# Retention and MLP on one core: the MLP's first layer by another seven-product form, with first products copied into PSUM banks

## The chip, the cores and the metric

The kernel runs on one core of a Trainium2 chip. A core has TensorE (matrix products, with a queue of its own for loading weights, shown as PEld), VectorE (DVE), ScalarE (ACT), GpSimd (POOL, which here issues the loads) and SyncE (SP, which here issues transposes by DMA and stores). Products are accumulated in PSUM, eight banks of 512 fp32 columns on 128 partitions; everything else lies in SBUF. The metric is the device time of one execution in microseconds, the median of several runs.

## The reference

The inputs are q, k and v of shape (8, 8, 576, 64): 8 batches, 8 heads, 576 positions, 64 columns a head. For each batch and head the reference computes retention: scores q k^T / 8, times a causal decay gamma_h^(i-j), times v. The heads' outputs are put side by side as x, 4608 tokens by 512, and go through an MLP:

```python
h = x @ w_in                       # 512 -> 2048
g = 0.5 * h * (1 + erf(h / sqrt(2)))
out = g @ w_out                    # 2048 -> 512
```

Inputs and output are fp32; the kernel casts to bf16 as it loads, and accumulates in fp32.

## The kernel before

**Attention.** The 576 positions of a batch are cut into four chunks of 128 and a tail of 64. A unit is one chunk of one batch, or the tails of two; there are 36, four to a block of 512 tokens, nine blocks (t = 0 to 8). A unit's q and k are transposed, by TensorE (`qk_ps`) for the first ten and by DMA (`qkT`) for the others; scores (`sc`) are masked on VectorE (`ret`) and multiplied by v or by v scaled by decay (`vh`) into `o_ps`; a running state `u_ps`, copied to `u_sb`, carries earlier chunks. VectorE writes the result into `xT`, the MLP's input. These products use part of the array, and are gathered into stretches of TensorE's order; APART lists groups of units whose scores get a stretch of their own.

**First layer.** For block 0 and 1 plain products: `hT` = w_in^T xT, 16 strips of 128 hidden columns, cut by tokens. From block 2 on (UNIT_FROM) the hidden dimension is cut into four quarters `kp`. A quarter pairs 256 columns of the lower half of the hidden dimension with 256 of the upper half, for all 512 tokens. LAYOUTS says of each block which quarters are computed plainly ("p3": 16 products of 512 columns, through four `hT` banks and four Gelus), and which by seven products of half-size blocks in place of eight (a digit; two digits: two quarters in turns; `unit_of`, `unit`, L1134). A product of the seven is four instructions of 256 columns. Before, 23 quarters of 28 go by seven.

In the form before, the left sums of w_in (`wi_sum`, five a quarter) and the right sums of x (`xs`, five a block) are made by VectorE. The seven products go to three banks a quarter: Y (products 3 and 5), Z (2, 4, 7) and X (1, 6). Between them stand a copy of product 3 (`third`, to `q`), q - Z (`less`), X + q (`more`), a copy of Y (`raw12`), q = X - copy (`dif`), and Z + q (`c11`), each on VectorE but for the copies, which take either engine; ScalarE then makes four Gelus out of PSUM (`quadrant`). BEHIND tells which product waits for which of these.

**Second layer.** Block 0 is plain (`oT`). From block 1 on (FAST) it goes by seven products too, over four hidden quarters at a time, in the order SECOND. Sums of g (`s`) and of w_out (`w_sum`) are made by VectorE. Product 1 is copied out (`first_of`, L1235, to `q` in SBUF) before product 2 adds onto it in its bank A; product 6 is formed in bank B, and VectorE adds the copy of product 1 to it there (`onto`, L1243); ScalarE's copies and VectorE's adds (`out_of`, `out_plus`) put the four parts into `o_sb`, which is stored.

**What sets the order.** Everything is recorded by a planner in the kernel (`Plan`, and the loop at the end): each piece of work has an engine, a planned duration, what it depends on and a due time; the planner steps through time, takes for each engine the piece that can start first (by due time among equals), and records it. The chip then runs each engine's queue in that order. For TensorE it chooses among attention work, macros (attention stretches, at need + SHIFT) and the next LOOK products of the MLP's stream. `bank` gives out the PSUM bank that is free earliest. While planned time is under 16 us, gaps on TensorE are filled with products of zeros (`warm`, after N_WARM of them at the start). ORDER is the order of the first loads on POOL's queue: q, k, v of a unit, `wi` and `wo` for strips of w_in and w_out. The first chunk's q, k and v come uncast by SyncE's and ScalarE's queues, and are cast by VectorE or ScalarE.

Of the kernel before, what the change touches and what calls it, by code (L numbers as in the profile page):

```python
# [14 lines left out]
NEVER = 1e9  # L15
# [92 lines left out]
def kernel(  # L108
# [52 lines left out]
    def slot_of(i):  # L161
# [15 lines left out]
    SLACK = 0.2  # L177
    CUTS = (0, 128, 256, 384, 512)
    AHEAD = 6
    WIDE = [2, 10, 14, 12, 4]  # L180
    VH_DUE = 14.0
# [4 lines left out]
    GAP_A = 4.7  # L186
    GAP_B = 0
    SHIFT = {4: -0.5, 5: 4.0, 6: 4.5, 7: -2.0, 8: 6.0, 9: 0.5, 10: 0.5, 11: -6.0, 12: -3.5, 13: -0.5, 14: -3.5, 15: -0.5, 16: -4.5, 17: -2.0, 18: -3.5, 19: 0.0, 20: 1.0}
    APART = [3, 5, 6, 7]
    BEFORE = 8.1  # L190
# [4 lines left out]
    LEAD = 8.9  # L195
    SPREAD = 5.6
    EASE = 9
# [24 lines left out]
    T = P.T  # L222
    add = P.add
# [25 lines left out]
    held = set()  # L249

# [32 lines left out]
    f_ring, m_ring, xs_ring = Ring(2), Ring(N_Q), Ring(1)  # L283
# [45 lines left out]
    W0 = 14.0  # L329
# [15 lines left out]
    for nm, src, eng, tag in (("q", q, nc.sync, "t"), ("k", k, nc.scalar, "t"), ("v", v, nc.sync, "o0")):  # L345
        t = first[nm] = (o_pool if nm == "v" else f_pool).tile([128, H, D], FP32, tag=tag, name=f"{nm}32")
        eng.dma_start(t, src[0, :, 0:C, :].rearrange("h s d -> s h d"))
# [247 lines left out]
    def turn(i, jj):  # L595
        b, t = st[i]["tr", jj] = bank([128, HP, 128], BF16, "qk_ps")
# [25 lines left out]
    def scores(i):  # L622
        if i in old:
            qkT = qkT_of(i)
            got = [bank([128, HP, 128], FP32, f"sc{e}") for e in range(2)]
            for hp in range(HP):
                for e in range(2):
                    sl = slice(64 * e, 64 * e + 64)
                    product(got[e][1][:, hp, :], lhsT=qkT[sl, 1, hp, :], rhs=qkT[sl, 0, hp, :],
                                     start=True, stop=True)  # L630
        else:
            qkT, n = qkT_of(i), i - slot_of(i)
            got = [bank([128, HP, 128], FP32, f"sc{e}") for e in range(2)]
            for hh in range(HP):
                h = 4 * n + hh
                for half in range(2):
                    out_ = slice(64 * half, 64 * half + 64)
                    for e in range(2):
                        sl = slice(64 * e, 64 * e + 64)
                        product(got[e][1][out_, hh, :], lhsT=qkT[sl, 1, h, out_], rhs=qkT[sl, 0, h, :],  # L640
                                         start=True, stop=True)
# [18 lines left out]
    def inner(i):  # L660
# [3 lines left out]
        s["o"] = bank([128, HP, 128], FP32, "o_ps")  # L664
# [15 lines left out]
    def state(bp, ci):  # L680
        if ci == 0:
            u_bank[:] = bank([128, H, D], FP32, "u_ps")
# [25 lines left out]
    def scores_atoms(n, b):  # L708
        qkT, sc, rows = qkT_of(n), st[n]["sc", b][1], half(b)
        if n in tails:  # L710
            return [(N64, [(sc[rows, h, :], qkT[rows, 1, h, :], qkT[rows, 0, h, :], True, True)]) for h in range(H)]
        return [(N64, [(sc[half(t), h, :], qkT[rows, 1, h, half(t)], qkT[rows, 0, h, half(t)], True, True) for t in range(2)])
# [53 lines left out]
    def weave(names):  # L766

        for nm in names:
            kind, key = key_of(nm)
            n = key[0]  # L770
            for b in {"both_": (1, 0), "odd_": (1,), "even_": (0,)}.get(kind, ()):
                if n in tails and ("sc", 1 - b) in st[n]:
                    st[n]["sc", b] = st[n]["sc", 1 - b]
                else:
                    st[n]["sc", b] = bank([128, H, 64], FP32, f"sc{b}")
            if kind in ("in_a", "in_t"):
                st[n]["o"] = [bank([128, HP, TAIL if n in tails else 128], FP32, "o_ps") for _ in range(2)]
            if kind == "st_a" and key[1] == 0:
                u_bank[:] = bank([128, H, D], FP32, "u_ps")
# [197 lines left out]
    BANK_OF = {"3": "Y", "5": "Y", "2": "Z", "4": "Z", "7": "Z", "1": "X", "6": "X"}  # L977
    LEFT = {"2": 0, "1": 1, "5": 2, "6": 3, "7": 4}
    RIGHT = {"3": 0, "1": 1, "4": 2, "6": 3, "7": 4}
# [59 lines left out]
    def wi_sum(kp, which):  # L1039
        if kp // 2 not in first_again:  # L1040
            first_again[kp // 2] = g_pool.tile([128, 2, 4, 2, 256], BF16, tag=f"first{kp // 2}", name="wi_sum")
        if kp not in wi_sums:
            wi_sums[kp] = (first_again[kp // 2][:, kp % 2],
                           const.tile([128, 2, 256], BF16, name=f"wi_sum{kp}"))
        a1, a2 = w_in_sb[kp], w_in_sb[kp + 4]
        a11, a12, a21, a22 = a1[:, 0:2], a1[:, 2:4], a2[:, 0:2], a2[:, 2:4]
        x0, x1, op = ((a21, a22, ALU.add), (a11, a22, ALU.add), (a11, a12, ALU.add), (a21, a11, ALU.subtract),
                      (a12, a22, ALU.subtract))[which]
        nc.vector.tensor_tensor(wi_sums[kp][0][:, which] if which < 4 else wi_sums[kp][1], x0, x1, op=op)

    def x_sum(t, which):
        if which == 0:
            xs_ring.take()
            xs_tiles[t] = xs_pool.tile([128, 5, 2, HALF], BF16, tag="xs", name="xs")
        x = x_of(t)
        b11, b12, b21, b22 = x[:, 0:2, :HALF], x[:, 0:2, HALF:], x[:, 2:4, :HALF], x[:, 2:4, HALF:]
        x0, x1, op = ((b12, b22, ALU.subtract), (b11, b22, ALU.add), (b21, b11, ALU.subtract), (b11, b12, ALU.add),
                      (b21, b22, ALU.add))[which]
        nc.vector.tensor_tensor(xs_tiles[t][:, which], x0, x1, op=op)

    def unit_left(kp, p, m):
        cols = slice(128 * m, 128 * m + 128)
        if p == "3":
            return w_in_sb[kp][:, 0:2, cols]
        if p == "4":
            return w_in_sb[kp + 4][:, 2:4, cols]
        n = LEFT[p]
# [595 lines left out]
```

## Time and profile before

| | |
|---|---|
| median of 3 runs | 281.41 us (281.37 to 281.67) |
| profiled execution, its span from first to last instruction | 279.2 us (the profile gives no other time of it) |
| instructions in the span | 8727 |
| TensorE busy | 273.0 us, 3626 products |
| VectorE busy | 228.7 us, 437 instructions |
| ScalarE busy | 181.7 us, 446 instructions |
| GpSimd busy | 110.4 us |
| granted TensorE clock, mean | 1.000 |

The page gives busy time by engine, then 40 slices of the span with the busy tenths of each engine, the granted clock and the DMA load, then the chain of waits: from the last instruction back to whatever released it, with the time of each piece. The groups of instructions have a count, the union of their busy time, the mean of one, and the idle time before them with what ended it. Because products are pipelined, the duration of one (273 ns for 256 columns) is longer than the slot that it takes in the stream; slots are read as the distance of starts, in the timeline or in the chain. All products are recorded by one helper, line 231 (transposes at 235), so groups go by tile names: `hT` plain first layer, `yT`, `zT`, `xT_` the seven-product banks, `oT` second layer, `sc`, `o_ps`, `u_ps` attention, `warm` the products of zeros. Copies on either engine are lines 573 and 575.

### The profile page before, as it was taken

The numbers are of one execution on the slowest core, as the hardware profiler recorded it, in microseconds if no ns is written. First come the engines' busy times: TensorE is split into PE (matmuls) and PEld (weight loads), VectorE is DVE, ScalarE is ACT, GpSimd is POOL, SyncE is SP. The second block draws the span as 40 slices with busy tenths as digits, with TensorE's granted clock in tenths as the row PEclk, the third lists the DMA queues.
The fourth block names the chain that finished last, engine by engine and source line by source line (L and its number), as shares of the span: only waits on it lengthen the run. The fifth ranks groups of instructions, "written<-read, shape, count | busy, mean of one in ns | idle before, by whom it ended". The sixth has DMA issues, their size and how long they took to land.

```text
span 279.2 us, 8727 instructions
## 1 busy us (share of the span) xinstructions
PE 273.0 (98%) x3626; PEld 216.2 (77%) x3626; DVE 228.7 (82%) x437; ACT 181.7 (65%) x446; POOL 110.4 (40%) x139
## 2 busy tenths in 40 slices
PE   7999999999999999999999999999999999999995
PEld 2675567478888688868886888778888888888684
DVE  5862554589989997999898999997899979969843
ACT  7766638786418823693559657975896689627840
POOL 8977688809755097311452725705000000000000
PEclk9999999999999999999999999999999999999999
DMA  9999999999999999999999999999600040003013
GB/s 150 161 187 179 190 175 173 178 169 165 149 142 177 193 134 151 134 236 99 142 197 88 128 160 222 116 113 121 190 2 2 6 151 2 2 22 131 0 40 113
DMA packets 152374, 35.55 MB, mean 127 GB/s; under 512 B 141072, under 2 KB 148240, under 8 KB 152336
## 3 DMA queue, kind: packets, MB, share of 16 engines
q0 software_dynamic: 115792, 17.97, 97.6%
q1 hardware_dynamic: 34544, 15.93, 31.0%
q10 hardware_dynamic: 2000, 1.11, 1.4%
q8 instruction: 28, 0.46, 0.7%
q14 instruction: 10, 0.08, 0.1%
HBM read 36.70 MB, written 9.44 MB: 165 GB/s over the span
## 4 chain that ended last, share of the span: by engine, by line
PE 79%; DMA 14%; POOL 5%; issue 1%; ACT 0%; DVE 0%; POOLq 0%
PE oT L231 37%; PE zT L231 11%; PE hT L231 9%; DMA w_out<-in_moe_w_out_dram 9%; PE yT L231 7%; PE o_ps L231 4%; DMA w_in<-in_moe_w_in_dram 3%; PE sc L231 2%; POOL qk_ld L522 2%; DMA qk_ld<-in_k_dram 2%; PE u_ps L231 2%; POOL w_in L528 1%; POOL v_ld L522 1%; PE xT__1851 L231 0%; PE xT__5150 L231 0%
## 5 line engine op out<-in xcount | busy, mean ns | idle before, releaser
L231 PEld LDWEIGHTS <-g 128*128 128x128 bf16 x576 | 55.2, 98 | 12.5 <-issue 0.4
L231 PEld LDWEIGHTS <-w_in 128*128 128x128 bf16 x528 | 47.2, 98 | 15.9
L231 PEld LDWEIGHTS <-wi_sum 128*128 128x128 bf16 x460 | 44.6, 98 | 7.1 <-issue 0.4
L231 PE MATMUL hT<-xT,w_in 128*128 128x256 bf16 (+2 forms) x344 | 49.0, 295 | 0.0
L231 PE MATMUL oT<-w_out,g 128*128 128x256 bf16 (+1 forms) x320 | 45.6, 294 | 0.1
L522 POOL DMA_DIRECT2D qk_ld<-in_q_dram x31 | 27.8, 898 | 38.9 <-DMA qkT<-qk_ld 24.2
L829 ACT ACTIVATE vh<-v_ld,dv 128x64 bf16<-128x64 bf16 x152 | 41.3, 348 | 1.0 <-DVE ret L657 1.0
L231 PEld LDWEIGHTS <-s 128*128 128x128 bf16 x384 | 36.8, 98 | 5.3 <-issue 0.4
L1104 ACT ACTIVATE g<-hT 128x512 bf16<-128x512 f32 (+1 forms) x58 | 31.5, 558 | 11.1 <-PE hT L231 10.4
L522 POOL DMA_DIRECT2D v_ld<-in_v_dram x31 | 28.0, 906 | 14.0 <-issue 6.7
L231 PE MATMUL oT<-w_sum,s 128*128 128x256 bf16 x256 | 32.6, 273 | 0.3 <-issue 0.3
L231 PE MATMUL oT<-w_sum,g 128*128 128x256 bf16 x256 | 31.1, 273 | 0.0
L1248 ACT COPY o_sb<-oT 128x512 f32<-128x512 f32 (+1 forms) x27 | 14.3, 539 | 23.7 <-PE oT L231 12.1
L522 POOL DMA_DIRECT2D qk_ld<-in_k_dram x31 | 28.0, 905 | 2.8 <-DMA v_ld<-in_v_dram 1.4
L1217 ACT ACTIVATE g<-zT 128x512 bf16<-128x512 f32 x46 | 26.4, 608 | 0.7 <-DVE zT L1226 0.6
L657 DVE TENSOR_TENSOR ret<-sc,msk 128x512 bf16<-128x512 f32 x36 | 22.9, 683 | 4.3 <-PE sc L231 4.3
L1252 DVE TENSOR_TENSOR o_sb<-o_sb,oT 128x512 f32<-128x512 f32 (+1 forms) x27 | 16.6, 626 | 10.5 <-PE oT L231 5.7
L834 ACT CAST u_sb<-u_ps 128x512 bf16<-128x512 f32 x19 | 11.3, 596 | 14.4 <-PE u_ps L231 12.5
L860 DVE TENSOR_TENSOR xT<-o_ps,dqT 128x512 bf16<-128x512 f32 x26 | 17.1, 683 | 1.9 <-PE o_ps L231 1.9
L573 DVE COPY qkT<-qk_ps 128x512 bf16<-128x512 bf16 x16 | 6.4, 421 | 13.9 <-PE qk_ps L235 13.8
L1226 DVE TENSOR_TENSOR zT<-q,zT 128x512 f32<-128x512 f32 x23 | 15.8, 692 | 2.1 <-PE zT L231 1.8
L575 ACT COPY q<-yT 128x512 f32<-128x512 f32 x16 | 9.0, 600 | 11.7 <-PE yT L231 11.7
(173 smaller groups left out, 470.6 us busy)
## 6 DMA issues: line engine op xcount, KB each, us to landing
out_dram<-o_sb SPq DMA_DIRECT2D x29, 256.0 KB, 3.4
qk_ld<-in_k_dram POOLq DMA_DIRECT2D x31, 128.0 KB, 7.2
qk_ld<-in_q_dram POOLq DMA_DIRECT2D x31, 128.0 KB, 7.5
v_ld<-in_v_dram POOLq DMA_DIRECT2D x31, 128.0 KB, 7.8
w_in<-in_moe_w_in_dram POOLq DMA_DIRECT2D x8, 256.0 KB, 8.1
w_out<-in_moe_w_out_dram POOLq DMA_DIRECT2D x8, 256.0 KB, 8.4
out_dram<-o_sb SPq DMA_DIRECT2D x7, 128.0 KB, 2.4
out_dram<-o_sb ACTq DMA_DIRECT2D x5, 128.0 KB, 1.9
```

The costliest lines, as they stand in the source:

```text
L231: return nc.tensor.matmul(*args, **more)
L522: nc.gpsimd.dma_start(dst, src[2 * bp + j, :, ci * C:ci * C + C, :].rearrange("h s d -> s h d"))
L575: nc.scalar.copy(dst, src)
L657: nc.vector.tensor_tensor(r, t, by, op=ALU.mult)
L829: nc.scalar.activation(vh[:, h], loaded[i][1][:, h], AF.Copy, scale=dv[:, h, ci:ci + 1])
L834: ins = (nc.vector.tensor_copy if engine == "dve" else nc.scalar.copy)(u_sb[t if bp >= FINE else ci % 2], u_bank[1])
L860: nc.vector.tensor_tensor(dst, o, dqT[:, :, ci * C:ci * C + C], op=ALU.mult)
L1104: nc.scalar.activation(g_of(t, m0)[:, m0 % 2:m0 % 2 + n, m0 // 8, lo:hi], hT, AF.Gelu)
L1217: nc.scalar.activation(target(key, what), chain[key][n][1], AF.Gelu)
L1226: nc.vector.tensor_tensor(to, chain[key]["q"], z, op=ALU.add)
L1248: nc.scalar.copy(target(key, what), chain[key][n][1])
L1252: nc.vector.tensor_tensor(to, to, chain[key][n][1], op=ALU.add)
```

## The change

The first layer's form is the one that the second layer has: its seven products are 1 and 2 (bank X), 6, 5 and 3 (bank Y), 7 and 4 (bank Z). Product 1 is copied from X into Y by ScalarE or VectorE (`seed`); products are then added onto the copy, without the start flag that would overwrite it: 6, after which Y is copied to SBUF (`aside`, u2), then 5, copied again (u4), then 3, which completes one part. Product 2 completes another in X. VectorE adds Z to u4 in SBUF after product 7, and u2 to Z in PSUM after product 4 (`plus`). ScalarE makes four Gelus, three from PSUM and one from SBUF.

[...] In the second layer product 1 is likewise copied into bank B in PSUM (L1235 before), and product 6 adds onto it; the adds of `onto` are gone.

The sums are four a quarter and four a block, each built from the one before. The quarters by seven are 27 of 28, N_T copies have a ring of six buffers, and the planner's numbers (VH_ACT, WIDE, SHIFT, APART, LOOK, HOLD, the due times) and the order of loads are new. The counts of instructions, from the two programs: 64 `hT` products of 512 columns fewer and 112 of 256 columns more; warming products of 512 columns 21 instead of 17, of 128 columns 11 instead of 13; VectorE 397 instead of 439, ScalarE 476 instead of 457; POOL and SyncE the same numbers in another order.

```diff
-    N_Q = 4
-    VH_ACT = [5, 6, 7, 8, 9, 10, 21, 22, 23, 24, 26, 27, 28, 29, 30, 31, 33, 34, 35]
+    N_T = 6
+    VH_ACT = [6, 8, 10, 11, 13, 15, 18, 19, 20, 21, 23, 25, 27, 28, 30, 31, 32, 34, 35]
-    N_WARM = 8
+    N_WARM = 7
...
-    APART = [3, 5, 6, 7]
+    APART = [3, 6, 7, 10, 11, 12]
...
-    LOOK = 12
-    HOLD = 6
-    LAYOUTS = {2: ['01', '2', 'p3'], 3: ['01', '2', 'p3'], 4: ['1', '02', 'p3'], 5: ['0', '1', '2', 'p3'], 6: ['01', '23'], 7: ['01', '23'], 8: ['0', '12', 'p3']}
+    LOOK = 18
+    HOLD = 20
+    LAYOUTS = {2: ['0', '1', '23'], 3: ['0', '1', '23'], 4: ['0', '1', '23'], 5: ['01', '23'], 6: ['01', '23'], 7: ['0', '1', '23'], 8: ['01', '2p3']}
...
-    ORDER = ("k2 k1 pos q1 wi0 q3 k3 q2 v1 v2 v3 wi4 wi7 wi1 wi5 v4 k4 q5 wi6 k5 wi3 wi2 q4 wo0 v5 wo4 wo1 q9 wo5 "
-             "q8 v7 wo6 v6 q7 q6 wo2 k7 v10 wo7 wo3 k6 q10 k8 v8 k10 k9 v9").split()
+    ORDER = ("q2 q1 v1 v3 k2 wi0 k3 pos q3 k1 wi4 v2 wi7 k4 wi3 k5 wi6 wi1 v5 wi5 q4 wi2 q8 q5 wo0 v4 wo4 q9 wo1 wo5 wo6 wo2 q10 wo7 v6 q6 wo3 k6 v7 q7 k8 k7 v9 v10 v8 k9 k10").split()
-    PRODUCTS = "3251467"
-    SECOND = "1267534"
+    PRODUCTS = '5167234'
+    SECOND = '1267543'
...
-    def bank(shape, dtype, name):
-        b = min((b for b in banks if b not in held), key=lambda b: free_at[b])
+    def bank(shape, dtype, name, fills, seeded=False):
+        got = [b for b in banks if b not in held and (b in filled or not seeded)]
+        b = min(got, key=lambda b: (max(free_at[b], T["now"]), not seeded and b in filled, free_at[b]))
         held.add(b)
+        (filled.add if fills else filled.discard)(b)
...
-    BANK_OF = {"3": "Y", "5": "Y", "2": "Z", "4": "Z", "7": "Z", "1": "X", "6": "X"}
+    BANK_OF = {"1": "X", "2": "X", "6": "Y", "5": "Y", "3": "Y", "7": "Z", "4": "Z"}
...
-    BEHIND = {"5": "m3", "4": "q", "6": "dif", "7": "c21"}
+    BEHIND = {"2": "seed", "6": "seed", "5": "u2", "3": "u4", "4": "c22"}
-    BEHIND2 = {"2": "p1", "5": "u2", "4": "p7"}
-    OPENS = "1673"
+    BEHIND2 = {"2": "p1", "6": "p1", "5": "u2", "4": "p7"}
+    OPENS = "173"
...
+    def seed(key, engine):
+
+        copy_on(engine, chain_of(key, 2, "Y", True), chain[key]["X"][1])
+
+    def aside(key, nm, engine):
         m_ring.take()
+        chain[key][nm] = f_pool.tile([128, 2, HALF], FP32, tag="t", name=nm, bufs=N_T)
+        copy_on(engine, chain[key][nm], chain[key]["Y"][1])
+
+    def plus(key, nm, into):
+        q_, z = chain[key][nm], chain[key]["Z"][1]
+        nc.vector.tensor_tensor(q_ if into == "q" else z, q_, z, op=ALU.add)
...
-    def onto(key):
-        x = chain[key]["B"][1]
-        nc.vector.tensor_tensor(x, x, chain[key]["p1"], op=ALU.add)
-        m_ring.give(T["dve"] + 0.12)
```

More of the change, by code (lines that the diff above doesn't have):

```diff
@@ L222 @@
     T = P.T
+    T["now"] = 0.0
     add = P.add
@@ L249 @@
     held = set()
+    filled = set()
     def nth_free(n):
@@ L282 @@
     s_ring = [Ring(1) for _ in range(2)]
[L283 removed]
+    m_ring, xs_ring = Ring(N_T), Ring(1)
     def laid(t, block):
@@ L624, in scores @@
             qkT = qkT_of(i)
-            got = [bank([128, HP, 128], FP32, f"sc{e}") for e in range(2)]
+            got = [bank([128, HP, 128], FP32, f"sc{e}", True) for e in range(2)]
             for hp in range(HP):
@@ new lines, in plus, with quadrant @@
+    def plus(key, nm, into):
+        q_, z = chain[key][nm], chain[key]["Z"][1]
+        nc.vector.tensor_tensor(q_ if into == "q" else z, q_, z, op=ALU.add)
+        if into != "q":
+            m_ring.give(T["dve"] + 0.12)
+    def quadrant(key, what):
+        n = {"c11": "X", "c12": "Y", "c21": "Z", "c22": "u4"}[what]
+        nc.scalar.activation(target(key, what), chain[key][n] if n == "u4" else chain[key][n][1], AF.Gelu)
+        if n == "u4":
+            m_ring.give(T["act"] + 0.14)
+        else:
+            release(chain[key][n][0], T["act"] + 0.14)
@@ new lines, in add_unit, with room @@
+        copy, act, dve = {"act": 0.5, "dve": 0.6}, 0.5, 0.6
+        def room(t=key[1], two=key[2] // 2):
+            return 0.0 if (t, two) in g_tiles else g_ring[two].at()
+        add(nm + "seed", "any", copy, pe["1"], lambda engine: seed(key, engine), due["1"] + 0.1, at=seed_room(key, "Y"))
+        add(nm + "u2", "any", copy, pe["6"], lambda engine: aside(key, "u2", engine), due["6"] + 0.1, at=m_ring.at)
+        add(nm + "u4", "any", copy, pe["5"], lambda engine: aside(key, "u4", engine), due["5"] + 0.1, at=m_ring.at)
@@ L1519, in warm @@
     def warm(gap):
-        b, t = bank([128, 512], FP32, "warm")
+        b, t = bank([128, 512], FP32, "warm", False)
         while gap > 0.0:
```

219 lines of the change are left out of this document (76 added, 143 removed).

## The prediction

> **What bounds the kernel now.** I read the page's head and slices first, then stretches, then the chain of waits, then the timeline around the places that the change touches.
>
> ```profile
> span 279.2 us, 8727 instructions
> PE 273.0 (98%) x3626; PEld 216.2 (77%) x3626; DVE 228.7 (82%) x437; ACT 181.7 (65%) x446; POOL 110.4 (40%) x139
> ...
> PE   7999999999999999999999999999999999999995
> ...
> DVE  5862554589989997999898999997899979969843
> ```
> ```profile
> 63.00:276.00 213.00, 212.50 (x2950) 178.23 (x2948) 190.95 (x337) 137.54 (x331) 64.34 (x78) 1.00 1.15 114
> ```
>
> TensorE has something to do in every slice. From 63 us to its last product it is busy 212.5 of 213.0 us (the row's columns are PE, PEld, DVE, ACT, POOL); VectorE, 191.0 us busy there, is the next fullest, ScalarE has 137.5. PEclk is 1.00. A busy PE need not be at its pace, so the pace is read from the chain of waits, where a piece is as long as the slots of its products:
>
> ```profile
> 48.04 5.75 DMA qk_ld<-in_k_dram
> ...
> 112.52 0.87 PE yT L231 x8
> ...
> 120.82 1.73 PE hT L231 x8
> ...
> 263.75 12.24 PE oT L231 x112
> ```
>
> A product of 256 columns takes 0.109 us (0.87/8, 12.24/112), one of 512 columns 0.216 (1.73/8). Where TensorE really stands still is told by its waits after 54 us and by its timeline:
>
> ```profile
> PE qk_ps L235 <- DMA qk_ld<-in_k_dram: 0.7, 1, 0.7
> PE oT L231 <- issue: 0.3, 1, 0.3
> PE zT L231 <- ACT g L1217: 0.2, 1, 0.2
> ```
> ```profile
> 1.19 5.09 PE L231 MATMUL warm<-u_sb 128*128 128x512 bf16 x8 [1.19 <-DVE ln_scale L352]
> ...
> 12.88 0.40 PE L235 MATMUL qk_ps<-ident,qk_ld 128*128 128x128 bf16 x4
> ...
> 16.23 0.74 PE L231 MATMUL o_ps<-ret,v_ld 128*64 128x128 bf16 x16
> ...
> 17.82 8.45 PE L231 MATMUL hT<-xT,w_in 128*128 128x128 bf16 x68
> ...
> 53.92 0.61 PE L235 MATMUL qk_ps<-ident,qk_ld 128*128 128x128 bf16 x8 [0.68 <-DMA qk_ld<-in_k_dram]
> ```
>
> So the time is the sum of TensorE's slots, plus the start (warming products until block 0 has scores and weights), plus one wait of 0.68 us for a k load that landed at 53.79 (48.04 + 5.75). Work taken off VectorE or ScalarE counts only through such waits.
>
> **The change, part by part.** Instructions are counted in the two programs.
>
> *Four more quarters by seven (23 to 27).* 64 products of 512 columns go, 112 of 256 come: 64 x 0.216 = 13.8 us against 112 x 0.109 = 12.2 us. **-1.6 us**, all of it on the path, since TensorE is.
>
> [...]
>
> *The new form's copies and sums.* VectorE loses 42 instructions: four sums a quarter become two, and nine adds of the second layer (oT<-oT,q) go; ScalarE gains 19. Each first product p1 is now copied from its bank X into bank Y, p6 adds onto it, the result is copied aside (u2), p5 adds on, is copied aside (u4), p3 adds on. So each quarter has three round trips from TensorE to a copy and back, 81 in all (52 copies on ScalarE, 29 on VectorE). What a trip takes is seen in the old form, where p5 waits for the copy of p3:
>
> ```profile
> 83.59 1.05 PE L231 MATMUL yT<-xs,w_in 128*128 128x256 bf16 x8
> ...
> 84.24 1.07 ACT L575 COPY q<-yT 128x512 f32<-128x512 f32 x2 [2.03 <-PE yT L231]
> ...
> 84.91 1.05 PE L231 MATMUL yT<-xT,wi_sum 128*128 128x256 bf16 x8
> ```
> ```profile
> L575 ACT COPY q<-yT 128x512 f32<-128x512 f32 x16 | 9.0, 600 | 11.7 <-PE yT L231 11.7
> ...
> L573 DVE COPY q<-yT 128x512 f32<-128x512 f32 x7 | 4.8, 682 | 0.0
> ```
>
> The first quarter's four slots end at 83.59 + 0.44 = 84.03, the dependent product starts at 84.91: 0.88 us with an idle ScalarE, and about 0.08 more by a VectorE copy (682 against 600 ns). In the new program I summed the products between producer and consumer: 24 of the 81 trips have two quarter products between (0.87 us), all of these on ScalarE; every VectorE trip has at least three (1.3 us). 57 trips are covered by other quarters' products; without that cover each would show its 0.88 us. The 24 tight ones lack 0.01 us when ScalarE is free. Its added 19 instructions at some 0.6 us make it about 11 us fuller, so I take 0.025 each, **+0.6 us**; ends 0 and 0.1 each (2.4 us, the copy as late as a VectorE one). The seed copy writes PSUM, for which before has no ScalarE row; nearest are 600 ns into SBUF and VectorE's two adds below, which differ by 10 ns, so I take 600. Behind a p6, p5 or p3 that waits stands all of TensorE's queue; a seed copy also waits for a free bank that a product has filled before, and behind it on ScalarE stand the Gelus that the second layer needs.
>
> ```profile
> L1226 DVE TENSOR_TENSOR zT<-q,zT 128x512 f32<-128x512 f32 x23 | 15.8, 692 | 2.1 <-PE zT L231 1.8
> L1196 DVE TENSOR_TENSOR q<-q,zT 128x512 f32<-128x512 f32 x23 | 15.1, 682 | 1.8 <-PE zT L231 0.8 <-ACT q L575 0.7
> ```
>
> In the second layer p6 now stands behind the p1 copies; the 16 products of p2 between (1.75 us) cover two copies, as they cover them for p2's own order now. The last product is p3 instead of p4 and its store goes by ScalarE's queue instead of SyncE's: nothing, as both are one add and one store.
>
> *Waits that go.* Two of the old order's holes lie in these stretches:
>
> ```profile
> 108.44 0.28 PE L231 MATMUL oT<-w_sum,s 128*128 128x256 bf16 x1
> 108.98 0.82 PE L231 MATMUL oT<-w_sum,s 128*128 128x256 bf16 x6 [0.26 <-issue]
> ...
> 171.04 0.60 PE L231 MATMUL xT__3421<-xs,wi_sum 128*128 128x256 bf16 x4
> 171.85 0.60 PE L231 MATMUL zT<-xs,wi_sum 128*128 128x256 bf16 x4 [0.21 <-ACT g L1217]
> ```
>
> One slot of 0.54 instead of 0.11, four of 0.81 instead of 0.44: 0.8 us. The second is the old form's p7 behind c21's Gelu, which the new form lacks; the first is a matter of order. **-0.8 us**, ends 0 and -0.8; what is late next is the tight trips above.
>
> *Attention groups.* With APART anew, two merged attention stretches after block 2 are split. The merged one below takes 0.82 us (125.08 to 125.90), its parts alone 0.37 (244.41 to 244.78) and 0.57 (93.73 to 94.30), and a break costs 0.10 (three 512-column slots from 124.33 end at 124.98): 0.2 us for this one, at most that for the other, **+0.3 us**.
>
> ```profile
> 93.73 0.64 PE L231 MATMUL sc<-qkT 64*64 64x128 bf16 x32
> 94.30 0.61 PE L231 MATMUL xT__1851<-xs,wi_sum 128*128 128x256 bf16 x4
> ...
> 124.33 0.81 PE L231 MATMUL hT<-xT,w_in 128*128 128x512 bf16 x3
> 125.08 0.32 PE L231 MATMUL o_ps<-ret,vh 64*64 64x64 bf16 x16
> ...
> 125.90 0.39 PE L231 MATMUL oT<-w_out,g 128*128 128x256 bf16 x2
> ...
> 244.41 0.32 PE L231 MATMUL o_ps<-ret,vh 64*64 64x64 bf16 x16
> ...
> 244.78 0.39 PE L231 MATMUL oT<-w_sum,g 128*128 128x256 bf16 x2
> ```
>
> *The start.* On POOL's queue the loads stand anew. The last chunk of block 0 waits for the seventh load now (q2, transposed at 12.88), for the ninth after (k1). POOL issues one in 0.9 us:
>
> ```profile
> 7.62 2.67 POOL L522 DMA_DIRECT2D v_ld<-in_v_dram  x3
> ...
> 13.81 2.72 DVE L657 TENSOR_TENSOR ret<-sc,near 128x512 bf16<-128x512 f32 x4
> ```
>
> The iota pos falls behind five more loads (4.5 us), and with it the decay factors and, behind them on ScalarE, the Gelu table load; the first Gelu needs block 0's first hT, which is later too, so I add nothing, and what it may cost lies in the end of +1.5. q's first cast changes place with k's between VectorE and ScalarE: one of 600 to 690 ns on each, as before.
>
> The last chunk's chain is 1.8 us later, and the four masks on VectorE, over at 16.53 now, at about 18.4. Behind the last mask now stand 16 o_ps, 8 hT and 16 u_ps, until 17.82; after, 8 o_ps only, until about 19.0 (one warming product less at first and five more later lie inside this). TensorE thus is 1.2 us late at the same point of work. Then comes the k load: it moves ahead of one v load and behind one k pair less, so I keep its landing to 0.2 us (53.6). Before that wait the new order places 24 products of 256 less and 8 of 512 more: 2.6 - 1.7 = 0.9 us less. TensorE reaches the wait near 52.9 as before, goes on at about 53.75 (53.92 now), but with 0.9 us more to do. **+0.7 us**; ends 0 (masks earlier, work found before the load) and +1.5 (the wait reached late).
>
> *Sum.* -1.6 + 0.6 - 0.8 + 0.3 + 0.7 = -0.8 us: span 278.4. The median of the runs shown, 281.41, is 2.2 above this execution's span; I keep that, so **280.6 us**. The likeliest case's own range is 279.9 to 281.3.
>
> **The rivals.**
> - *ScalarE late at the trips (slower).* Place: the 24 tight trips. At 0.1 us each and without the 0.8 us of waits that go, -1.6 + 2.4 + 0.3 + 0.7 = +1.8: 283.2 us. It ends slower once the trips lose over 0.08 us each beyond the rows (1.4 + 0.56 us over 24, from the sum without trips of -1.4). For it: four quarters in a row need 16 Gelus and some eight copies on ScalarE in 12 us of products, and 27 Gelus now read SBUF, where the row of 64 elements takes 348 ns against 604 for 512 and 385 for 256 from PSUM, whose slope gives 221 for 64. Against: the row at 84.24 and the 35% that ScalarE is idle. Chance 0.20.
>
> ```profile
> L829 ACT ACTIVATE vh<-v_ld,dv 128x64 bf16<-128x64 bf16 x152 | 41.3, 348 | 1.0 <-DVE ret L657 1.0
> ...
> L1104 ACT ACTIVATE g<-hT 128x512 bf16<-128x512 f32 x46 | 27.0, 604 | 9.9 <-PE hT L231 9.6
> ...
> L1104 ACT ACTIVATE g<-hT 128x256 bf16<-128x256 f32 x12 | 4.6, 385 | 1.2 <-PE hT L231 0.8
> ```
>
>  [...]
> - *The start is not late* and the trips cost nothing: -1.6 - 0.8 + 0.3 = -2.1, 279.3 us. For it: the k wait swallows lateness. Chance 0.18.
> - *The wait for k is reached late:* start +1.5, 281.4 us. Chance 0.13.
> - *The seven products are no cheaper.* By shares of busy time a 512-column hT product reads 0.237 us (28.4/120) and a 256-column one 0.138 (12.7/92): 112 x 0.138 - 64 x 0.237 = +0.3 instead of -1.6, 282.5 us. Against it stand the chain's slots. Chance 0.02.
>
> **How the numbers follow.** The likeliest case has 0.47. About 0.2% (0.56 us) is what a measurement of this kernel can tell from no change, so 280.85 to 281.97 counts as the same. Faster: three quarters of the likeliest and the 279.3 case, 0.53. Same: the rest of the likeliest and half of the late wait, 0.19. Slower: 0.28. The range 279.2 to 282.8 leaves out most of the 283.2 case and a tail below.
>
> **What would show it.** PE 512-column hT rows fall from 120 to 56; VectorE's busy time falls by some 25 us, ScalarE's rises by 10; TensorE's 24th 128-column hT of block 0 starts its successors near 19.0 instead of 17.82; the wait for k stays about 0.7 us; no yT product waits over 0.1 us on a copy. Wrong: waits of TensorE on ScalarE's copies of several us in all, or a first layer of block 0 that starts later than 19.5.

## The result and the profile after

The changed kernel takes 285.05 us, the median of 4 runs (284.95 to 285.30), against 281.47 for the kernel before in the same comparison (4 runs): a ratio of 1.0126, 95% interval 1.0111 to 1.0140. It is 3.6 us slower, where 0.8 us faster was predicted, and outside the range. Ratios, here and below, are of fast executions; one of the four of `old_start` below, the one whose profile is read, was slow by its clock (296.32 us), and its 290.78 and its points are too high for that.

The page of the changed kernel, its span, the busy time by engine, and TensorE's busy tenths:

```profile
span 282.7 us, 8764 instructions
PE 273.5 (97%) x3676; PEld 222.2 (79%) x3676; DVE 208.1 (74%) x395; ACT 192.3 (68%) x465; POOL 110.5 (39%) x139
...
PE   6899999999999999999999999999999999999994
```

VectorE lost 20.6 us of work and ScalarE gained 10.6, but TensorE still bounds the kernel. To see where its time went, each execution is cut where the second layer of block 1 begins (its first `oT` product of 256 columns). The stretches before and behind that point, first of the kernel before, then of the changed one; the columns are the length, then PE, PEld, DVE, ACT, POOL busy, the granted clock and the DMA load:

```profile
0.00:68.06 68.06, 65.52 (x774) 42.34 (x775) 42.37 (x109) 47.31 (x121) 51.17 (x68) 1.00 1.87 174
68.06:275.97 207.91, 207.44 (x2854) 173.82 (x2851) 185.89 (x328) 134.43 (x325) 59.28 (x72) 1.00 1.14 112
```
```profile
0.00:72.32 72.32, 67.03 (x777) 43.71 (x777) 44.38 (x115) 42.88 (x99) 53.46 (x71) 1.00 1.94 170
72.32:279.18 206.86, 206.47 (x2902) 178.46 (x2899) 163.33 (x280) 149.42 (x366) 57.03 (x70) 1.00 1.14 110
```

Behind the cut, where all quarters by seven lie, the change gains 1.05 us (207.91 to 206.86). Ahead of it, in attention and the plain products of blocks 0 and 1, it loses 4.26. So the loss isn't where the new form works. What stands there is in the waits of TensorE and in its timeline (in brackets the idle time ahead of a piece, and what ended it):

```profile
PE qk_ps L235 <- ACT qk_ld L582: 1.2, 1, 1.2
...
PE warm L231 <- ACT qkT L582: 0.5, 1, 0.5
PE oT L231 <- ACT qkT L582: 0.5, 1, 0.5
...
PE oT L231 <- DVE qkT L580: 0.4, 1, 0.4
PE hT L231 <- DVE qkT L580: 0.3, 1, 0.3
```
```profile
1.19 3.17 PE L231 MATMUL warm<-u_sb 128*128 128x512 bf16 x7 [1.19 <-DVE ln_scale L359]
...
20.52 3.84 PE L231 MATMUL hT<-xT,w_in 128*128 128x128 bf16 x56
24.20 0.61 PE L235 MATMUL qk_ps<-ident,qk_ld 128*128 128x128 bf16 x8
...
38.72 1.02 PE L231 MATMUL oT<-w_out,g 128*128 128x512 bf16 x4 [0.45 <-ACT qkT L582]
...
53.20 1.02 PE L231 MATMUL oT<-w_out,g 128*128 128x512 bf16 x4 [0.36 <-DVE qkT L580]
...
56.91 0.61 PE L235 MATMUL qk_ps<-ident,qk_ld 128*128 128x128 bf16 x8
```

A second-layer product of block 0 has no use for `qkT`, the copy of transposed q and k. It waits for that copy because it was given the bank that the transposes had just been written to. The choice of a bank is a part of the change. `filled` is the kernel's set of banks that products have written in full; a seed copy is given only a bank of this set. That a seed could not use another is not shown, as no run gives it one. For all other tiles, among banks that the plan holds free, `bank` now takes first one outside the set, and a bank that transposes were written to is such a bank. In the recorded programs, the number of tiles after a group of transposes until its bank is taken again, for the 20 groups in order:

```
before   8 9 8 8 9 8 9 10 7 7 7 7 4 4 3 3 4 4 6 6
changed  3 2 2 2 3 3 4  3 3 3 2 2 2 2 2 2 2 2 2 2
```

TensorE doesn't wait any more for the load of the last k, for which it waited 0.68 us before: it comes to that point at 56.91, 3 us later than before, with no idle time ahead of it.

### The profile page after: what moved, and what is told of

Read it like the earlier page. It is cut to its first block, busy times and chain, and to the rows that moved or that the text cites. A ratio compares the mean times of both kernels' runs of the same rounds, so it can differ in the third digit from the quotient of the medians.

```text
span 282.7 us, 8764 instructions
## 1 busy us (share of the span) xinstructions
PE 273.5 (97%) x3676; PEld 222.2 (79%) x3676; DVE 208.1 (74%) x395; ACT 192.3 (68%) x465; POOL 110.5 (39%) x139
## 4 chain that ended last, share of the span: by engine, by line
PE 93%; DMA 2%; POOL 1%; DVE 1%; issue 1%; ACT 1%; POOLq 0%; DVEq 0%
PE oT L231 40%; PE yT L231 13%; PE hT L231 11%; PE zT L231 9%; PE pT L231 8%; PE o_ps L231 5%; PE sc L231 3%; DMA qk_ld<-in_k_dram 2%; PE u_ps L231 2%; PE qk_ps L235 1%; PE warm L231 1%; POOL qk_ld L529 1%; POOL v_ld L529 1%; DVE qkT L580 0%; DVE ret L664 0%
## 5 line engine op out<-in xcount | busy, mean ns | idle before, releaser
L231 PEld LDWEIGHTS <-w_in 128*128 128x128 bf16 x604 | 54.7, 98 | 13.2 <-issue 0.4
L231 PEld LDWEIGHTS <-wi_sum 128*128 128x128 bf16 x432 | 42.0, 98 | 6.1
L231 PE MATMUL hT<-xT,w_in 128*128 128x256 bf16 (+2 forms) x280 | 34.4, 275 | 0.5 <-DVE qkT L580 0.3
L1102 ACT ACTIVATE g<-hT 128x512 bf16<-128x512 f32 (+1 forms) x42 | 22.4, 537 | 17.0 <-PE hT L231 16.5
L231 PE MATMUL yT<-xs,wi_sum 128*128 128x256 bf16 x216 | 30.6, 272 | 0.0
L231 PE MATMUL pT<-xT,w_in 128*128 128x256 bf16 x216 | 30.1, 273 | 0.0
L582 ACT COPY u<-yT 128x512 f32<-128x512 f32 x36 | 20.7, 589 | 6.8 <-PE yT L231 6.5
L1189 DVE TENSOR_TENSOR u<-u,zT 128x512 f32<-128x512 f32 x27 | 18.2, 683 | 5.3 <-ACT u L582 5.0
L580 DVE COPY qkT<-qk_ps 128x512 bf16<-128x512 bf16 x14 | 5.6, 421 | 21.1 <-PE qk_ps L235 21.1
L1189 DVE TENSOR_TENSOR zT<-u,zT 128x512 f32<-128x512 f32 x27 | 18.3, 690 | 2.9 <-PE zT L231 2.8
```

The source lines that it names most:

```text
L231: return nc.tensor.matmul(*args, **more)
L580: nc.vector.tensor_copy(dst, src)
L582: nc.scalar.copy(dst, src)
L1102: nc.scalar.activation(g_of(t, m0)[:, m0 % 2:m0 % 2 + n, m0 // 8, lo:hi], hT, AF.Gelu)
L1189: nc.vector.tensor_tensor(q_ if into == "q" else z, q_, z, op=ALU.add)
```

## The experiments

Times are medians; the kernel before, on the chips of these runs, has 280.92 to 281.14. Where a point inside an execution is given, it is TensorE's start of the 25th narrow (128-column) `hT` product (17.82 before, 20.52 changed) and of block 1's second layer (68.06 before, 72.32 changed).

**1. Bank or start.** Four kernels part the new choice of a bank from the new start (the order of loads and the numbers around it). `oldest_bank` puts the old choice into the changed kernel (the plan then also puts some instructions into another order, which the kernels of 2 exclude):

```diff
-        b = min(got, key=lambda b: (max(free_at[b], T["now"]), not seeded and b in filled, free_at[b]))
+        b = min(got, key=lambda b: free_at[b])
```

> The changed kernel, with banks given out by the earliest release again instead of first those that no product has filled. Theory A (the new choice hands the bank that a transpose has just left to the next product, which then waits for the copy out of it): the waits of TensorE on the copies of transposes (0.3 to 0.6 us each, 38.05 and 52.62 us in the changed kernel) go, 1.8 to 2.5 us less, 282.6 to 283.3 us. Theory B (the new order of loads makes the start late, and nothing else counts): 284.8 to 285.2 us. Theory C (the new form's copies cost it): 284.8 to 285.2 us.

`old_start` keeps the new choice, and puts back the old start:

```diff
-    N_WARM = 7
-    SLACK = 0.01
+    N_WARM = 8
+    SLACK = 0.2
...
-    AHEAD = 21
-    WIDE = [6, 2, 10, 12, 4]
-    VH_DUE = -0.8
+    AHEAD = 6
+    WIDE = [2, 10, 14, 12, 4]
+    VH_DUE = 14.0
...
-    ORDER = ("q2 q1 v1 v3 k2 wi0 k3 pos q3 k1 wi4 v2 wi7 k4 wi3 k5 wi6 wi1 v5 wi5 q4 wi2 q8 q5 wo0 v4 wo4 q9 wo1 wo5 wo6 wo2 q10 wo7 v6 q6 wo3 k6 v7 q7 k8 k7 v9 v10 v8 k9 k10").split()
+    ORDER = ("k2 k1 pos q1 wi0 q3 k3 q2 v1 v2 v3 wi4 wi7 wi1 wi5 v4 k4 q5 wi6 k5 wi3 wi2 q4 wo0 v5 wo4 wo1 q9 wo5 "
+             "q8 v7 wo6 v6 q7 q6 wo2 k7 v10 wo7 wo3 k6 q10 k8 v8 k10 k9 v9").split()
...
-    W0 = 6.8
+    W0 = 14.0
```

> The changed kernel with the old numbers of the start: order of loads, warming products, the strips done 512 wide, look-ahead, first due times. Theory B: the 25th product of block 0's first layer begins near 17.8 instead of 20.5 us, and the whole gains 2.7 us, 282.0 to 282.6 us. Theory A alone: no more than 0.5 us faster, 284.5 to 285.1, as the waits after transposes stay. Theory C: 284.5 to 285.3 us.

`old_start_oldest_bank` has both edits, and `old_form_new_start` is the kernel before with the second edit the other way round.

> Both of these edits: the new form and 27 quarters, with the old start and banks by the earliest release. Theories A and B together: the start of the kernel before, and the gain of 1.0 us that the changed kernel shows from the second layer of block 1 on: 280.2 to 280.8 us. Theory C: above 282 us, with a gain of less than 0.3 us after block 1.

> The kernel before (old form, 23 quarters, banks by the earliest release) with the new numbers of the start. Theory B: 281.4 + 2.7, less up to 1.1 us of waits that lateness swallows: 283.0 to 284.2 us. Theories A and C: 281.2 to 281.8 us.

| | time, us | ratio to before (95%) | 25th narrow `hT` | block 1's second layer |
|---|---|---|---|---|
| `oldest_bank` | 280.91 | 1.0002 (0.9983 to 1.0020) | 19.53 | 68.64 |
| `old_start` | 290.78 | 1.0337 (1.0293 to 1.0381) | 21.81 | 73.26 |
| `old_start_oldest_bank` | 284.96 | 1.0151 (1.0117 to 1.0185) | 17.98 | 67.92 |
| `old_form_new_start` | 283.71 | 1.0095 (1.0067 to 1.0123) | 19.36 | 68.47 |

The choice of a bank carries the whole loss: without it 3.5 us are back (ratio 1.0002 against 1.0126), more than was expected. All the waits of TensorE that the list has for `oldest_bank`, then where the second of them and the last k's transposes stand:

```profile
PE warm L231 <- DVE ln_scale L359: 1.2, 1, 1.2
PE qk_ps L235 <- DMA qk_ld<-in_k_dram: 0.8, 1, 0.8
PE o_ps L231 <- DVE ret L664: 0.4, 1, 0.4
PE oT L231 <- issue: 0.2, 1, 0.2
```
```profile
11.13 0.40 PE L235 MATMUL qk_ps<-ident,qk_ld 128*128 128x128 bf16 x4 [0.81 <-DMA qk_ld<-in_k_dram]
...
53.61 0.61 PE L235 MATMUL qk_ps<-ident,qk_ld 128*128 128x128 bf16 x8
```

No wait on a copy of transposes is left. The 0.8 us are for k2 of block 0, which the new order loads fifth instead of first; at the last k's transposes, 53.61, TensorE doesn't wait. The two kernels with the old start missed the times expected from the theories A and B: 67.92 shows that the old start does what it did, but the rest of the new plan, made for another start, then takes `old_start_oldest_bank` 211.3 us from block 1's second layer to TensorE's last product, where the kernel before takes 207.9. Its time alone would fit theory C, but behind that point TensorE waits 2.2 us for masks of the attention (`ret`) and 0.2 for a copy. `old_form_new_start` met its number by another way than expected: at block 1's second layer it is only 0.41 us late (68.47), and loses the rest later. A start taken from one plan into another says little about the whole; the points inside say more.

**2. Where the choice costs.** `rule_after_block1` has the new choice only from planned time 72 us on. Every engine's instructions and their order are those of the changed kernel, only banks differ:

```diff
-        b = min(got, key=lambda b: (max(free_at[b], T["now"]), not seeded and b in filled, free_at[b]))
+        b = min(got, key=lambda b: (max(free_at[b], T["now"]), not seeded and b in filled, free_at[b]) if T["now"] > 72 else (free_at[b],))
```

> The preference for banks that no product has filled is applied only once the plan is past 72 us; until then a bank is the one released earliest. Every engine's instructions and their order are those of the changed kernel; only banks differ. Theory A (the 4 us are products of the first 72 us that begin on a bank which transposes have just left, and so wait for the copy out of it): 280.4 to 281.6, with no wait of TensorE on a copy of the transposes in the chain of waits. Theory C (banks handed on too early cost all along the kernel): 282.5 to 284, with the markers of the first 72 us earlier by less than 2 us or the end giving the gain back.

`rule_not_transposes` keeps the choice but treats a bank left by transposes as filled (`leftT` is the set of such banks); `late_release` changes only when the plan holds that bank free:

```diff
+        b = min(got, key=lambda b: (max(free_at[b], T["now"]), not seeded and (b in filled or b in leftT), free_at[b]))
```
```diff
-        release(b, T[engine] + 0.05)
+        release(b, T[engine] + 0.65)
```

> The preference stays all along, but a bank that transposes left counts as filled when a bank is chosen. Theory A: 280.4 to 281.8, as with the earliest-released bank everywhere. Theory C: 283 to 284.5, since scores, outputs and narrow products still hand their banks on.

> The preference stays as it is, but the plan reckons the bank of transposes free 0.65 us after the copy out of them instead of 0.05. Instructions and their order are those of the changed kernel; the next tile on such a bank is then the second to sixth taken after it, where it was the second to fourth. If the plan's short margin is what makes the waits: 281 to 282.5. If the margin matters little, since the plan's copy ends earlier than the chip's by more than 0.6 us, or since others of the short handovers cost: 283 to 285.

`rule_in_before` puts the new choice into the kernel before and changes nothing else (the calls tell which tiles fill a bank); its instructions and their order are those of the kernel before:

```diff
-        b = min((b for b in banks if b not in held), key=lambda b: free_at[b])
+        b = min((b for b in banks if b not in held), key=lambda b: (max(free_at[b], T["now"]), b in filled, free_at[b]))
+        (filled.add if fills else filled.discard)(b)
...
```

> The kernel before, its seven products, quarters and numbers untouched, with the new choice of a bank alone. Theory A: 4 us slower at most and 2 at least, 283.0 to 285.5, with waits on copies of the transposes in the chain of waits and most of the loss by 72 us. Rival D (the choice costs only beside the new order of loads and the new start): 280.8 to 282.

| | time, us | ratio to before (95%) | 25th narrow `hT` | block 1's second layer |
|---|---|---|---|---|
| `rule_after_block1` | 281.38 | 1.0014 (0.9988 to 1.0040) | 19.33 | 68.43 |
| `rule_not_transposes` | 282.98 | 1.0079 (1.0056 to 1.0102) | 20.86 | 70.88 |
| `late_release` | 283.80 | 1.0103 (1.0076 to 1.0129) | 22.21 | 72.04 |
| `rule_in_before` | 288.31 | 1.0283 (1.0242 to 1.0324) | 21.31 | 72.54 |

With the same instructions in the same order, other banks in the first 72 us are worth 3.2 us (ratio 1.0014 against 1.0126), and 3.9 us at block 1's second layer; behind 72 us the choice costs nothing that these runs can tell. In the kernel before, the choice alone makes 7.3 us, more than expected: 4.5 of them stand by block 1's second layer, and in the profiled execution 1.7 more are one stop at 79 us for which the profile shows nothing to wait for. But transposes are only a part of it: without their banks 282.98 remain, over what theory A gave (281.8) and at the lower end (283) of theory C.

`late_release` by its time (283.80) says that the plan's short margin matters little; its profile says otherwise for the transposes. At the 25th narrow product it is 1.69 us behind the changed kernel, mainly because its products ran at half the pace from 9.81 us on (last section). At block 1's second layer it is 0.28 ahead. Of the 1.97 us that it wins in between, 1.57 are at the three places (34.40, 38.72 and 53.20 us) where the changed kernel waits for copies of transposes. These waits are gone; all that its list shows of waits for `qkT` or a Gelu stands before 17 us:

```profile
PE warm L231 <- ACT qkT L582: 0.5, 1, 0.5
PE warm L231 <- ACT g L1102: 0.3, 1, 0.3
```

**3. The first products.** In the runs with the new choice, the first products of zeros, each given a bank of its own, ended at 4.4 us instead of 5.6, and TensorE then stood for 1.2 us. Was that the rest of the loss? `warm_one_bank` gives them one bank, `warm_one_bank_not_transposes` adds the edit of `rule_not_transposes`, and `ten_first_products` has ten of them in separate banks:

```diff
-        b, t = bank([128, 512], FP32, "warm", True)
+        t = ps.tile([128, 512], FP32, tag=banks[0], name="warm")
...
-        release(b, 0.0)
+    filled.update(banks[:N_WARM])
```
```diff
-    for _ in range(N_WARM):
+    for _ in range(10):
```

> The changed kernel, its seven first products of zeros all in one bank instead of one bank each; instructions, their order and all later banks as the changed kernel's. In the five profiles with one bank these products begin 0.64 us apart and end at 5.64; in the five with separate banks they begin 0.43 us apart, end at 4.4, and TensorE then waits 1.2 us for the cast of q or idles later. Theory D (the 4 us have two parts: the early end of the first products, and the transposes' banks): the first part is what the run without the transposes' part still lost, 277.82 - 275.16 = 2.66 us at TensorE's end, so 281.8 to 283.0 here, first products 0.64 us apart. Theory A alone (transposes' banks are all): 284.5 to 285.4.

> Both parts undone, the preference kept for everything else. Theory D: 280.3 to 281.5, the time with the earliest-released bank everywhere. If a third place of the preference costs: over 282.

> The changed kernel with ten first products of zeros instead of seven, still in separate banks, the plan told the same end. They would end at 1.2 + 10 x 0.43 = 5.5, where seven in one bank end at 5.64. If what costs is that TensorE stands idle early: 281.8 to 283.2, as with one bank. If it is the banks themselves: 284.5 to 285.4.

The times, in this order, are 284.68 (ratio 1.0110, 1.0073 to 1.0147), 283.19 (1.0067, 1.0047 to 1.0088) and 283.86 (1.0101, 1.0069 to 1.0133). The first row of TensorE's timeline, of `warm_one_bank` and of `ten_first_products`:

```profile
1.19 4.45 PE L231 MATMUL warm<-u_sb 128*128 128x512 bf16 x7 [1.19 <-DVE ln_scale L359]
```
```profile
1.19 4.24 PE L231 MATMUL warm<-u_sb 128*128 128x512 bf16 x10 [1.19 <-DVE ln_scale L359]
```

The first products now end at 5.64 and 5.43, yet the 25th narrow `hT` starts at 20.44 and 20.46 (20.52 changed). Theory D falls: the next piece waits for the cast of q until 5.58 in any case, and TensorE's idle time there was no loss. The third time lies between its two ranges and meets neither; it can't be told from the changed kernel's, as the intervals overlap (1.0111 to 1.0140).

**4. The other places.** A comparison of start times, product by product, of `rule_not_transposes` and `rule_after_block1` shows the lag growing in two kinds of steps: 0.1 to 0.3 us where a tile begins behind products of zeros, and 0.19 us at every second tile of narrow `hT` products. In the programs both have a reason. A gap's products of zeros don't count as filling their bank, so the next tile gets that very bank, and TensorE waits for its own last product to be finished (seven tiles in `rule_not_transposes`, none in `rule_after_block1`). A narrow `hT` tile doesn't fill its bank either, so these tiles take two banks in turn and nearly each waits for the Gelu of the last but one, while other banks stand free:

```
the seven narrow hT tiles from 20.5 us (19.5) on: bank, and what the program waits for
changed      3 4 3 4 3 4 3   (all but one on the Gelu of a tile just ahead)
oldest_bank  2 1 7 6 5 4 0   (on older Gelus and products)
```

Three kernels except the places one by one: `passed` is the set of banks left by tiles of the names given, and these count as filled when a bank is chosen; the three have ("qk_ps", "warm"), ("qk_ps", "hT") and all three names.

```diff
+        b = min(got, key=lambda b: (max(free_at[b], T["now"]), not seeded and (b in filled or b in passed), free_at[b]))
+        (passed.add if name in ('qk_ps', 'warm', 'hT') else passed.discard)(b)
```

> The preference is withheld from banks left by transposes and by the products of zeros that fill gaps; narrow first-layer products still hand theirs on. Theory E (the 4 us have three places, all before 72 us: transposes, products of zeros, and narrow first-layer products that take two banks in turn): the fillers' share is the steps of 0.12 to 0.26 us at seven tiles that begin on a bank of the filler just ahead, some 1.1 us of the 2.0 that the run without the transposes' part lost: 281.3 to 282.4. Theory A alone: 282.6 to 283.4.

> The preference is withheld from banks left by transposes and by first-layer products of one slot of tokens; fillers still hand theirs on. Theory E: the narrow products' share is six steps of 0.19 us between 19 and 24 us, 1.1 us: 281.3 to 282.4, and in the timeline the 56 narrow products follow each other without the steps. Theory A alone: 282.6 to 283.4.

> The preference is withheld in all three places and kept for the rest. Theory E: 280.3 to 281.5, the time with the earliest-released bank. A fourth place: over 281.8.

| | time, us | ratio to before (95%) | 25th narrow `hT` | block 1's second layer |
|---|---|---|---|---|
| `not_transposes_not_fillers` | 282.51 | 1.0049 (1.0031 to 1.0067) | 20.18 | 70.19 |
| `not_transposes_not_narrow` | 281.41 | 1.0022 (1.0004 to 1.0040) | 20.09 | 69.19 |
| `not_any_of_three` | 281.15 | 0.9998 (0.9981 to 1.0015) | 19.41 | 68.51 |

`not_transposes_not_fillers` missed its range by 0.1 us and the fillers' share is smaller than expected; the other two kernels lie in theirs. At block 1's second layer the shares add up: transposes 72.32 - 70.88 = 1.44, fillers 70.88 - 70.19 = 0.69, narrow tiles 70.88 - 69.19 = 1.69, together 3.82, and 72.32 - 68.51 = 3.81. No fourth place is left. These points are of one execution each: 0.36 of the transposes' 1.44 are a stop at 60.78 us inside a group of scores of the changed kernel, for which the profile shows nothing to wait for and which `ten_first_products`, 71.87 us at block 1's second layer, doesn't have. Without it the transposes' share is 1.1 and the whole 3.5. The narrow tiles' six steps of 0.19 make 1.1 of their 1.69; most of the rest, 0.45, stands at a filler at 15.23 us that got such a bank. How the narrow tiles lose it is seen in the timeline, of `not_transposes_not_narrow` first (TensorE and ScalarE), then ScalarE of the changed kernel at the same work:

```profile
20.09 3.30 PE L231 MATMUL hT<-xT,w_in 128*128 128x128 bf16 x56
...
20.75 3.06 ACT L1103 ACTIVATE g<-hT 128x256 bf16<-128x256 f32 x7
```
```profile
22.24 0.83 ACT L1102 ACTIVATE g<-hT 128x256 bf16<-128x256 f32 x2 [0.25 <-PE hT L231]
23.32 0.38 ACT L1102 ACTIVATE g<-hT 128x256 bf16<-128x256 f32 x1 [0.25 <-PE hT L231]
```

56 narrow products take 3.30 us with seven Gelus in one row behind them; with two banks in turn they take 3.84 (20.52 above), and the two engines wait for each other. No such wait stands in the list of waits, since each is under what the list shows: the 0.5 us appear only as a longer row, three steps of 0.18 in seven tiles.

**5. Two terms of the prediction.** Both kernels start from `oldest_bank`; the first has the LAYOUTS of the kernel before (23 quarters by seven), the second the first twelve loads in the old order (the same twelve):

```diff
-    ORDER = ("q2 q1 v1 v3 k2 wi0 k3 pos q3 k1 wi4 v2 wi7 ...
+    ORDER = ("k2 k1 pos q1 wi0 q3 k3 q2 v1 v2 v3 wi4 wi7 ...
```

> The changed kernel with the earliest-released bank and with the 23 quarters by seven that the kernel before has, 4 fewer. By the prediction's term (1.6 us for 4 quarters of 64 columns in 32 fewer products each): 281.9 to 283.2 beside 280.9 for 27 quarters. If quarters by seven gain nothing because tighter waits take it: 280.5 to 281.4.

> The changed kernel with the earliest-released bank, the first twelve loads in the order that the kernel before has, the rest as changed. By the prediction's start term (0.7 us, made by the order of the first loads): 279.8 to 280.6 where the earliest-released bank alone has 280.9, with the 25th narrow product before 18.5 us. If the load of the last k, which lands at 53.6 whatever comes first, holds the resume at 53.75: 280.6 to 281.3, with a longer wait for that load.

23 quarters take 284.15 us (1.0103, 1.0066 to 1.0139), more than expected. The stretch behind the cut and the two largest waits in it, of `oldest_bank_23_quarters`, then the stretch of `oldest_bank`:

```profile
68.51:278.94 210.43, 208.37 (x2846) 173.83 (x2851) 152.53 (x262) 149.43 (x364) 60.90 (x74) 1.00 1.13 110
...
PE oT L231 <- ACT oT L582: 1.3, 2, 0.8
```
```profile
68.64:275.16 206.52, 206.47 (x2901) 178.36 (x2899) 162.53 (x279) 149.76 (x367) 59.01 (x72) 1.00 1.19 112
```

TensorE's busy time, which can hide short waits, is 1.9 us more with four quarters fewer, near the 1.6 of the term; the other 2.0 are idle time, most of it behind copies, in a plan whose numbers were not made for these quarters.

The old first loads gave 280.95 us (0.9999, 0.9980 to 1.0017). Their 25th narrow `hT` starts at 17.68, as before the change, and then:

```profile
53.73 0.61 PE L235 MATMUL qk_ps<-ident,qk_ld 128*128 128x128 bf16 x8 [0.67 <-DMA qk_ld<-in_k_dram]
```

Here TensorE comes earlier and the last k holds it until 53.73; in `oldest_bank` it came at 53.61, behind its own work. Block 1's second layer starts at 68.76, against 68.64. A start 1.9 us earlier gains nothing.

## Why the prediction was wrong

- *The step that failed* is the list of parts: it had no term for the new choice of a bank. The prediction named the banks once, "a seed copy also waits for a free bank that a product has filled before", and looked only at who is given a filled bank, not at who is sent to the others. The missing term is +3.5 us at block 1's second layer (3.8 with the stop at 60.78): 1.1 transposes, 0.69 products of zeros, 1.69 narrow tiles. It could have been seen in the two programs: the tiles between transposes and the next use of their bank fall from between 3 and 10 to between 2 and 4, and the trip from TensorE to a copy and back, 0.88 us, was in the prediction's own rows.
- *What bounds the kernel*: right. TensorE is busy 206.47 of 206.86 us behind the cut.
- *Four more quarters, -1.6*: right within what the runs tell (-1.9 of TensorE's busy time).
- *Trips, waits and attention groups, +0.6 - 0.8 + 0.3*: with the quarters -1.5 for the part behind the cut; it measured -1.05 in the changed kernel, -1.39 in `oldest_bank`. Their single sizes were not told apart. The copies take what was assumed, by rows of the changed kernel:

```profile
L582 ACT COPY yT<-pT 128x512 f32<-128x512 f32 x16 | 9.0, 577 | 9.4 <-PE pT L231 6.3 <-DVE xs L1062 1.7 <-ACT vh L836 1.3
...
L580 DVE COPY yT<-pT 128x512 f32<-128x512 f32 x11 | 7.6, 694 | 1.5 <-ACT g L1195 0.9 <-PE pT L231 0.6
...
L1195 ACT ACTIVATE g<-u 128x512 bf16<-128x512 f32 x27 | 17.1, 651 | 0.0
```

- *The rival of a late ScalarE*: out. Behind the cut no product of the seven starts over 0.1 us later than its slot, though in the changed kernel a Gelu from SBUF (`u`, above) takes 651 ns against 609 to 616 from PSUM (`pT`, `zT`, `yT`).
- *The start, +0.7*: right in size once the choice of a bank is undone, but in part by chance. Predicted was 68.06 + 0.7 = 68.76; the three kernels without the loss have 68.43, 68.51 and 68.64. The resume agrees only as a number: predicted was a load that holds TensorE until 53.75, and `oldest_bank` comes there at 53.61 behind its own work, its 25th narrow product 1.7 us late instead of 1.2. (Before, TensorE came to the wait at 53.92 - 0.68 = 53.24, not near 52.9.) The other half holds: from there it needs 15.03 us to the cut, against 14.14 before, the "0.9 us more to do". The order of loads, which the prediction told at length, makes the first layer late but has no part in the 0.7, as the run with the old first loads shows.
- *The k wait reached late* (281.4) came about, but by 3 us and by the banks; the prediction's own sign of being wrong, a first layer later than 19.5, came with it (20.52).
- *The sum*: the profiled execution of `oldest_bank` has a span of 278.5 us, near the predicted 278.4. That is chance, as the kernel before has spans of 278.3 to 279.7 in the same comparison. The median equals that of the kernel before (ratio 0.9983 to 1.0020), so the 0.8 us of gain are not borne out in time even there.

## What to carry to other kernels

A rule that chooses buffers for one purpose also decides who gets the rest: when a choice prefers some banks, count for each kind of tile how many tiles pass until its bank is taken again, before and after, and compare that with the time of a copy or a Gelu. Short handovers need not show in the list of waits; they show as the same products taking longer in the timeline (here 56 narrow ones 3.84 us instead of 3.30), so compare two executions start by start, at fixed points of the work. A planner's numbers belong together: pieces of one plan put into another lost 2.8 to 4.0 us against the kernel before (`old_form_new_start`, `old_start_oldest_bank`, `oldest_bank_23_quarters`), for reasons of their own.

## What the runs showed of the hardware

The first products of 512 columns start 0.43 us apart when each has a bank of its own and 0.64 when all have one (3.17 us for seven against 4.45), in all the 18 profiles of this case. In the program, a product that opens a bank last written by TensorE waits for that product to be finished; the 0.21 us between the two paces are this wait. 0.43 is still twice the later 0.216. The granted clock reads 1.00 in the rows of that time, but no trace has a record of the clock before 4.1 us (the changed kernel's first is at 9.15), and a stretch without a record reads 1.00.

On record a low clock stands in the first 13 us of two of the 18 profiles, 0.50 for 3.41 us: in `not_any_of_three` from 7.51 us on, in `rule_in_before` from 9.11. Two stretches of `rule_in_before` (the clock is the last but two column), then four products of 512 columns and one of 128, merged into one row with the form of the first, in `not_any_of_three` and in `late_release`:

```profile
6.50:8.00 1.50, 0.62 (x10) 0.34 (x10) 1.07 (x2) 1.36 (x4) 1.50 (x3) 1.00 2.37 158
...
10.00:12.00 2.00, 1.94 (x18) 1.07 (x17) 1.39 (x3) 0.85 (x3) 2.00 (x4) 0.50 2.43 154
```
```profile
8.80 2.02 PE L231 MATMUL warm<-u_sb 128*128 128x512 bf16 x5
```
```profile
9.81 1.97 PE L231 MATMUL warm<-u_sb 128*128 128x512 bf16 x5 [0.50 <-ACT qkT L582]
```

Under the recorded 0.50, products of 512 columns start 0.43 us apart (8.80, 9.23, 9.65 and 10.08 in `not_any_of_three`), and so they do in `late_release` (10.19, 10.62 and 11.04), which has no record of its clock before 13.65. The first products of all the kernels have this pace too, where each has a bank of its own; that their clock is 0.50 is likely from that, but not on record. In `rule_in_before` one such stretch can cost at most 1.7 us, half its length, of the 7.3. What brings it isn't shown. In `rule_in_before` it follows a pause (TensorE busy 0.62 of 1.50 us from 6.5 on), but `ten_first_products` was busy for 0.58 of 2.00 us from 8 on, and its clock stayed at 1.00, on record from 4.66.

Some executions hold a single stop of 1.3 to 1.6 us near 110 us, ahead of the same attention product, for which the profile shows nothing to wait for; in `not_any_of_three`:

```profile
109.26 0.36 PE L231 MATMUL o_ps<-qkT,u_sb 64*64 64x128 bf16 x11 [1.27 <-issue]
```

It was in three of the 18 profiles, in five others the same stop took 0.4 to 0.9 us, and in ten there was none. What makes it is open, and so is whether it is why the faster kernels' times spread over 2 us.
